# A linear-attention and expert kernel on one core: TensorE's idle products taken out, their PSUM bank given to short products, and a new written-out order of the work

## The chip, the cores and the metric

The kernel runs on one core of a Trainium2 chip. The metric is device time in microseconds. The runs of the kernel before took 575.65, 576.88 and 577.29 us (median 576.88). An execution taken with the profiler took 577.56 us, of which its trace spans 575.7 us.

The engines are named as in the profile: PE is TensorE (PEld its weight loads), DVE is VectorE, ACT is ScalarE, POOL is GpSimd, and SP is SyncE, whose queue issues nearly all transfers.

## What is computed

```python
# q, k, v, alpha: (4, 8, 768, 48); state: (4, 8, 48, 48)
for t in range(768):
    state = alpha[:, :, t, :, None] * state + einsum('bhd,bhe->bhde', k[:, :, t], v[:, :, t])
    y[:, :, t] = einsum('bhd,bhde->bhe', q[:, :, t], state)
x = y.transpose(0, 2, 1, 3).reshape(3072, 384)
g = x @ w_gate                       # 384 x 1536
out = (g / (1 + exp(-g)) * (x @ w_val)) @ w_out
```

The three weight matrices come as 64-bit floats. The kernel cuts them down to 32 bits on the chip.

## The kernel before

**Attention.** The 3072 rows of four batches are worked off in 16 units of 192 time steps (all 8 heads), three chunks of 64 in each. For a unit `u`, words name the steps: `La`, `Lk`, `Lq` and `V` load alpha, k, q and v; `G` and `f` are the backward and the forward scan over alpha on VectorE (with `z` clearing some columns between two units); `mk` and `q` multiply k and q by the decays; `S` are the scores on TensorE, `ma` their causal masks on VectorE; `K` brings k to rows by TensorE transposes (copied out of PSUM by `kc` on ScalarE) in units 0 to 3, and `kr` does the same on VectorE in units 4 to 15; `B` (or `Bw`) makes the carried state, `ad` adds it up, `de` decays it for the next unit; `Y` is the output, rounded to a high part by `yh` and its rest by `yl`. In units 0 to 3 the inputs are turned on TensorE: `p` widens a tile, `T` transposes it into two PSUM banks, and `ea`, `ek`, `cq` copy it out; from unit 4 on VectorE turns them (`tr` for alpha, `tk`, `tq`). `R` and `x` bring the output of units 0 and 1 into the layout of the second part, and from unit 2 on `xr` does it by transfers.

**Experts.** Two units give a block of 384 rows, eight blocks in all. A step is one block and one slice of 128 of the 1536 hidden columns: `g` and `v` are nine products each (three slices of the contraction, times high and low parts), `sl` is the activation on ScalarE, `h` the product with `v` on VectorE, `hh` and `hl` its high and low parts, and `o` nine products into the output. Steps 0 to 6 are block 0, slices 0 to 6; steps 7 to 13 are block 1 with the same slices, and so the same weights; then come the remaining five slices of both, and from step 24 on block after block. `g` and `v` have one PSUM bank each, so `v` of a step waits until `h` of the step before has read that bank.

**Weights.** Group `n` is loaded by `wl`, cut to 32 bits by three VectorE instructions (`w..v0` to `v2`, lines 149, 152 and 155), and split into a high part (`w..a`) and its rest (`w..p`, line 326 on VectorE or GpSimd). Groups 0 to 2 hold one piece, the others two. The cut goes through one of three buffers `t`. Later `wr` and `wc` load and check the ranges of the weights, and `Lc` and `ck` those of alpha.

**The order** of all this is written out as a table: the string `ORDER` is a list of words `engine:name@banks`, and each engine gets its instructions in the order of its words (`t` TensorE, `v` VectorE, `s` ScalarE, `g` GpSimd, `y` SyncE). An engine works its list off in order, and the framework adds the waits that the data and the buffers ask for. The figures behind `@` choose the PSUM banks out of `BANKS`. Of eight banks, three are for short products (`A0` to `A2`), three for the output `o` (`ops0` to `ops2`) and one each for `v` and `g`; until they have their own work, short products use all but `ops2`.

**Idle products.** In `ops2`, before the first `o` needs it, the words `t:3+` or `t:1*` put products of zeros on TensorE, whose result is never read: `dummy32` on 32-bit zeros, `dummy` on 16-bit ones. They stand between the real products of the first units; there are 11 of the first kind and 20 of the second.

Of the kernel before, what the change touches and what calls it, by code (L numbers as in the profile page):

```python
# [48 lines left out]
s:kc1.2 y:wl8 s:kc1.1 v:w3v0 s:qc1 t:4* t:S1@34 v:w3v1 s:ad0.2 v:w3v2 y:wl9 s:ea2 v:de1 s:ad0.0 t:1+ t:3* t:Ta3@02
v:G2 s:kc1.0 t:Y0@16 y:wl10 s:pk2 s:w3a v:f2 g:z2 t:Bw1@5 s:yh0.0 y:V2 s:yh0.1 s:vc1 v:yl0.0 g:w3p s:ad1.0 v:ma1.0  # L50
s:ad1.1 v:ma1.2 v:yl0.1 t:1+ t:2* t:Tk2@14 g:pq2 v:ma1.1 t:R0.2@6 g:w2a v:mk2 s:ad1.2 s:x0.2 v:w2p t:Y1@35 v:w4v0
v:w5v0 t:Tq2@14 v:w5v1 y:V3 s:yh1.0 t:R0.1@6 s:yh1.1 v:w6v0 s:cq2 v:w4v1 s:pk3 t:3* t:K2.1@1 v:w4v2 t:R0.0@4 s:x0.1
s:kc2.1 t:K2.0@6 v:yl1.1 g:q2 s:w4a t:K2.2@1 v:x0.0 v:yl1.0 t:Tk3@45 s:kc2.0 y:Lq3 v:de2 s:kc2.2 y:wl11 t:R1.1@3 s:ea3
t:R1.2@6 v:w6v1 y:wl12 t:R1.0@1 v:w6v2 s:x1.2 t:S2@02 s:vc2 y:wl13 v:G3 t:Bw2@6 s:x1.1 y:wl14 s:x1.0 s:pq3 v:ma2.2
g:qc2 y:Lk4 v:mk3 t:Tq3@13 g:w4p s:ad2.0 s:ad2.1 v:ma2.1 v:ma2.0 v:w7v0 s:ad2.2 v:w7v1 y:wl15 t:Y2@02 v:w7v2 s:cq3
v:de3 s:w7a y:wl16 t:g0 v:f3 g:z3 s:yh2.0 s:yh2.1 s:vc3 t:K3.1@1 t:v0 y:wl17 s:sl0 v:yl2.0 g:q3 s:kc3.1 v:yl2.1 t:g1
y:xr2 v:h0 s:hh0 v:w7p s:qc3 t:S3@01 v:w5v2 s:sl1 t:K3.2@2 v:ma3.2 g:hl0 t:K3.0@3 s:w5a t:v1 v:ma3.1 s:kc3.0 v:ma3.0
s:w6a v:w5p t:o0 s:kc3.2 v:w8v0 v:w6p t:Bw3@0 v:h1 v:w9v0 s:hh1 v:w10v0 y:wl18 t:g2 v:w10v1 s:ad3.0 s:ad3.1 v:w8v1
y:V4 t:v2 s:sl2 v:w8v2 v:w9v1 s:w8a t:Y3@01 v:w9v2 t:g3 v:w8p s:w9a y:V5 s:yh3.0 v:w11v0 s:yh3.1 v:h2 g:hl1 v:yl3.0
t:v3 s:hh2 g:w9p v:yl3.1 s:sl3 v:tk4 t:o1 y:xr3 g:hl2 v:h3 t:g4 s:hh3 v:w12v0 s:vc4 v:hl3 v:w12v1 t:v4 s:sl4 v:w12v2  # L60
t:g5 v:h4 v:w11v1 t:o2 s:sl5 v:w11v2 y:La4 v:w10v2 s:w12a t:o3 s:hh4 v:w12p y:La5 s:w10a t:v5 v:hl4 s:w11a v:w10p t:o4
v:w13v0 v:w13v1 t:g6 v:w13v2 v:h5 g:w11p s:w13a t:v6 s:sl6 v:tr4 s:hh5 g:hl5 t:g7 v:h6 y:Lq4 v:w14v0 s:hh6 t:v7
v:w15v0 s:sl7 v:w15v1 t:o5 v:w13p v:h7 g:hl6 t:g8 s:hh7 v:w14v1 t:o6 v:w14v2 s:sl8 v:w15v2 s:w14a t:v8 s:ot6.0 v:w16v0
s:ot6.1 y:os6.0 v:w16v1 y:os6.1 t:g9 v:h8 g:hl7 s:hh8 v:w16v2 t:v9 s:sl9 v:hl8 s:w16a v:G4 t:g10 s:ot6.2 y:os6.2 t:o7
v:f4 g:z4 s:sl10 t:o8 v:h9 g:mk4 t:v10 s:hh9 g:hl9 v:tq4 t:g11 g:w15a v:h10 y:Lk5 t:o9 s:sl11 g:w15p v:kr4.0 s:hh10
v:kr4.1 t:v11 g:hl10 v:kr4.3 t:g12 g:q4 v:h11 v:kr4.2 s:hh11 t:v12 s:sl12 g:hl11 s:qc4 v:tr5 t:S4@01 g:w16p t:B4@2
v:h12 y:Lq5 v:ma4.2 g:w14p t:o10 v:tk5 s:ad4.0 v:ma4.1 t:o11 y:La6 s:hh12 v:ad4.1 g:hl12 v:ma4.0 t:g13 v:ad4.2 v:w17v0
t:o12 s:sl13 v:w17v1 y:wl19 v:w18v0 t:v13 v:w18v1 v:w18v2 t:Y4@01 v:h13 v:w17v2 s:hh13 t:g14 s:yh4.0 y:V6 v:G5 s:w17a
s:yh4.1 t:v14 s:sl14 v:de5 s:vc5 v:yl4.1 g:hl13 t:g15 v:h14 g:w18a v:yl4.0 s:hh14 t:o13 s:sl15 v:mk5 v:kr5.3 g:hl14
t:v15 s:ot13.0 s:ot13.1 g:w18p v:kr5.0 y:os13.1 t:g16 y:os13.0 v:h15 v:kr5.1 s:hh15 g:w17p t:v16 s:sl16 v:kr5.2 t:g17  # L70
g:hl15 v:h16 v:tq5 s:ot13.2 t:v17 s:sl17 v:f5 g:z5 y:Lk6 t:g18 y:os13.2 t:o14 y:pl18.0 v:h17 v:q5 t:v18 s:hh16 v:w19v0
v:w19v1 v:hl16 t:S5@01 y:xr4 v:w19v2 s:sl18 v:tr6 g:qc5 t:o15 g:w19a g:w19p v:ma5.2 t:o16 s:hh17 v:h18 v:hl17 t:B5@1
v:tk6 s:hh18 g:hl18 t:o17 v:ma5.0 v:ad5.0 y:La7 v:ad5.1 t:o18 v:G6 t:g19 y:Lq6 v:ot18.0 g:mk6 v:ma5.1 t:v19 s:sl19
y:pl18.1 v:ad5.2 y:os18.0 t:g20 v:kr6.3 v:h19 t:Y5@01 v:kr6.1 s:sl20 s:hh19 g:hl19 v:kr6.0 t:v20 s:yh5.0 y:V7 s:vc6
v:de6 t:g21 s:yh5.1 v:ot18.1 v:yl5.1 v:h20 v:tq6 s:sl21 t:v21 s:hh20 y:pl18.2 g:hl20 y:os18.1 v:yl5.0 t:g22 y:Lk7
v:h21 v:f6 g:z6 t:v22 s:sl22 y:xr5 t:g23 v:h22 g:q6 v:kr6.2 t:v23 v:ot18.2 g:qc6 v:tr7 t:o19 v:G7 t:o20 s:hh21
y:os18.2 y:pl23.0 v:tk7 g:hl21 t:S6@01 s:hh22 t:B6@2 g:hl22 s:sl23 v:ma6.2 y:La8 g:mk7 v:h23 t:o21 v:ma6.1 v:ad6.0
y:Lq7 t:o22 v:ma6.0 s:hh23 v:kr7.0 g:hl23 t:g24 v:kr7.2 v:f7 g:z7 t:o23 s:sl24 t:v24 v:ot23.0 v:kr7.3 y:os23.0 t:g25
# [1029 lines left out]
```

## Time and profile before

| what | value |
|---|---|
| median of the runs | 576.88 us |
| the profiled execution, its time | 577.56 us |
| the same, its span in the trace | 575.7 us |
| granted TensorE clock, mean | 0.994 |
| DVE busy over the span | 386.3 us in 596 instructions |
| ACT busy over the span | 248.5 us in 573 instructions |
| POOL busy over the span | 146.4 us in 169 instructions |

A row of the trace in order of time has a start and a length in us, the engine, the line of the program, the operation and its tiles, how many instructions were merged, and in brackets how long the engine idled before and what ended that. A row of a grouped view has busy time in all, the mean of one instruction in ns, and the idle time ahead of the group. A row of a table of stretches has the length and the busy us of each engine in it, the granted TensorE clock, the share of the transfer engines and GB/s. Products on TensorE overlap, so that one's length is more than the distance to the next.

### The profile page before, as it was taken

Reading aid. Unit: us, or ns where it says so; the run is one execution under the profiler, and the core shown is the slowest. Engines: PE = TensorE matmul, PEld = TensorE weight load, DVE = VectorE, ACT = ScalarE, POOL = GpSimd, SP = SyncE. Lnnn points to the kernel's source line nnn. Section 1 sums busy time; section 2 is a strip of 40 time slices with the busy share of each in tenths; the row PEclk is TensorE's granted clock in tenths of the full one; section 3 lists DMA queues with packets and bytes.
Section 4 is the critical chain, followed back from the end, with each engine's and each line's share of the span. In section 5 each row is a group of like instructions: output and inputs, shape, how many; then the busy total and the mean of one; then the engine's idle time right before and its main releaser. Section 6 shows DMA issues by size and latency. Waiting matters only on the chain.

```text
span 575.7 us, 13792 instructions
## 1 busy us (share of the span) xinstructions
PE 556.7 (97%) x5552; PEld 529.0 (92%) x5552; DVE 386.3 (67%) x596; ACT 248.5 (43%) x573; POOL 146.4 (25%) x169
## 2 busy tenths in 40 slices
...
GB/s 205 276 327 219 269 120 142 59 87 98 93 144 155 140 128 105 124 79 149 153 185 198 165 183 135 164 125 125 174 134 126 121 152 66 100 77 48 1 0 47
DMA packets 95367, 77.66 MB, mean 135 GB/s; under 512 B 32832, under 2 KB 92224, under 8 KB 95296
## 3 DMA queue, kind: packets, MB, share of 16 engines
...
## 4 chain that ended last, share of the span: by engine, by line
PE 83%; DMA 8%; SPq 3%; DVE 2%; issue 1%; ACT 1%; DVEq 0%; ACTq 0%
PE ops L735 25%; PE v L703 25%; PE g L703 24%; DMA raw<-in_moe_w_gate_dram 4%; PE A L558 2%; PE s L534 2%; PE y L630 2%; DMA V<-in_v_dram 1%; DMA Le<-in_q_dram 1%; PE y L613 1%; DMA raw<-in_moe_w_val_dram 1%; PE y L614 1%; SPq L687 1%; SPq L281 1%; DVE t L152 1%
## 5 line engine op out<-in xcount | busy, mean ns | idle before, releaser
L703 PE MATMUL v<-xT,w 128*128 128x384 f32 x864 | 167.7, 338 | 2.8 <-DVE h L715 2.8
L703 PE MATMUL g<-xT,w 128*128 128x384 f32 x864 | 167.2, 337 | 0.9 <-ACT h L711 0.9
L735 PE MATMUL ops<-w,hh 128*128 128x384 f32 x576 | 159.0, 338 | 0.3 <-ACT K L498 0.3
L703 PEld LDWEIGHTS v<-xT,w 128*128 128x128 f32 x864 | 150.5, 188 | 4.7 <-DVE h L715 3.9
L703 PEld LDWEIGHTS g<-xT,w 128*128 128x128 f32 x864 | 150.9, 188 | 2.0 <-ACT h L711 1.4
L724 POOL TENSOR_TENSOR hl<-h,hh 128x384 fp32r<-128x384 f32 x67 | 70.6, 1053 | 249.5 <-ACT hh L719 241.7
L715 DVE TENSOR_TENSOR h<-h,v 128x384 f32<-128x384 f32 x96 | 52.9, 551 | 117.8 <-PE v L703 104.5
L719 ACT CAST hh<-h 128x384 fp32r<-128x384 f32 x96 | 49.0, 512 | 150.3 <-DVE h L715 76.7
L735 PEld LDWEIGHTS ops<-w,hh 128*128 128x128 f32 x576 | 105.4, 188 | 1.3 <-ACT K L498 0.6
L735 PE MATMUL ops<-w,hl 128*128 128x384 f32 x288 | 96.8, 336 | 0.0
L711 ACT ACTIVATE h<-g 128x384 f32<-128x384 f32 x96 | 47.0, 489 | 112.2 <-PE g L703 101.0
L509 DVE STREAM_TRANSPOSE K<-Gs 32x384 f32<-32x384 f32 x96 | 54.7, 570 | 5.4 <-PE A L558 3.7
L735 PEld LDWEIGHTS ops<-w,hl 128*128 128x128 f32 x288 | 54.1, 188 | 0.0
L449 DVE TENSOR_TENSOR_SCAN AT<-AT,back 128x771 f32<-128x771 f32 x16 | 29.2, 1824 | 0.7
L440 DVE TENSOR_TENSOR_SCAN Gs<-AT,inj 128x772 f32<-128x772 f32 x16 | 29.4, 1837 | 0.3
L568 DVE TENSOR_TENSOR X<-s,mask 64x384 f32<-64x384 f32 (+1 forms) x48 | 26.0, 551 | 4.8 <-PE s L534 4.2
L724 DVE TENSOR_TENSOR hl<-h,hh 128x384 fp32r<-128x384 f32 x29 | 16.0, 556 | 16.3 <-ACT hh L719 16.2
L453 POOL MEMSET AT<- 128x3 f32 x16 | 1.7, 105 | 90.3 <-DVE AT L449 90.3
L298 ACT ACTIVATE wc<-wc,wbias 128x384 f32<-128x384 f32 x36 | 23.3, 648 | 1.2
L326 POOL TENSOR_TENSOR w<-t,w 128x768 fp32r<-128x768 f32 (+1 forms) x11 | 19.1, 1741 | 15.3 <-ACT w L322 15.1
L468 POOL TENSOR_TENSOR X<-trq,AT 112x768 f32<-112x768 f32 x11 | 19.3, 1752 | 13.4 <-ACT trq L799 6.4
L558 PE MATMUL A<-V,K 64*48 64x48 f32 (+1 forms) x720 | 21.4, 207 | 0.1
...
## 6 DMA issues: line engine op xcount, KB each, us to landing
...
```

The lines of the kernel that those rows point to most:

```text
L298: nc.scalar.activation(dev, dev, AF.Relu, bias=wbias, scale=-1.0, accum_out=wviol[:, 0, i : i + 1])
L440: nc.vector.tensor_tensor_scan(*(x.rearrange("p g t -> p (g t)")[:, ::-1] for x in (Gs, AT, inj)), 0.0, op0=ALU.mult, op1=ALU.add)
L449: nc.vector.tensor_tensor_scan(Af, Af, back[:, 1 : n + 1], back[:, 0:1], op0=ALU.mult, op1=ALU.add)
L509: nc.vector.transpose(out=bass.AP(k0.tensor, k0.offset, [k0.ap[0], (G * 2 * D, NU), (2 * D, G), (1, 32)]), in_=Kg[j * BO + x : j * BO + x ...
L558: nc.tensor.matmul(to[j * BO : j * BO + D, g - gs.start, :], Ks[r, x, g, KC[j]], Vd[r, x, g, VC[j]], start=(x == 0 or not whole), stop=(x ...
L568: nc.vector.tensor_tensor(out=X[r, z, f * GF : (f + 1) * GF, :].rearrange("r g (c t) -> r g c t", c=NU), in0=sps[f][r].rearrange("r g (c t ...
L703: nc.tensor.matmul(pt, wsp[kind, f][a][:, kt * P : (kt + 1) * P], xT[blk][:, b_, kt, :], start=(n == 0), stop=(n == 3 * KT - 1),)
L711: nc.scalar.activation(h, acc.pop(("g", blk, f)), AF.Silu)
L715: nc.vector.tensor_tensor(out=h, in0=h, in1=acc.pop(("v", blk, f)), op=ALU.mult)
L719: nc.scalar.copy(out=hh, in_=acc["h", blk, f])
L724: eng.tensor_tensor(out=hl, in0=acc.pop(("h", blk, f)), in1=hh.bitcast(F32), op=ALU.subtract)
L735: nc.tensor.matmul(ops[blk][i], h[b_][:, i * P : (i + 1) * P], wsp["o", f][a], start=(first and n == 0), stop=(last and n == 2),)
```

## The change

The idle products go: both helpers, the words for them, and the zeros' two names. The bank `ops2` becomes the eighth entry of `BANKS`, so that short products may name it; three do. The string `ORDER` is a new one throughout. No other function changes; lines behind the removed ones move up by 2, and later by 13 to 16.

```diff
 ORDER = """
-y:La0 y:wl0 y:wl1 y:Lq1 y:La1 y:Lq0 y:Lk0 s:pa0 y:V1 t:3+ t:1* t:Ta0@01 v:w0v0 v:w0v1 s:ea0 v:w0v2 v:w1v0 v:w1v1 s:w0a
+y:La0 y:wl0 y:Lk2 y:La2 y:Lq0 y:La1 y:V0 s:pa0 t:Ta0@01 v:w0v0 v:w0v1 s:ea0 v:w0v2 g:w0a v:G0 y:Lk0 s:pq0 y:Lq1 y:V1
...
-    busy32 = inj[:, 0, 0:P]
-    busy = busy32.bitcast(BF16)
...
-    early_ps = ps.tile([P, 512], F32, tag="ops2", name="early_ps")
-
-    def dummy(n):
-
-        for _ in range(n):
-            nc.tensor.matmul(early_ps, busy[:, 0:P], busy.unsqueeze(1).to_broadcast([P, 2, 2 * P]), start=True, stop=True)
-
-    def dummy32(n):
-        for _ in range(n):
-            nc.tensor.matmul(early_ps, busy32[:, 0:P], busy32.unsqueeze(1).to_broadcast([P, 4, P]), start=True, stop=True)
...
-    BANKS = ("A0", "A1", "A2", "ops0", "ops1", "vps", "gps")
+    BANKS = ("A0", "A1", "A2", "ops0", "ops1", "vps", "gps", "ops2")
...
-            if name[-1] in "*+":
-                (dummy32 if name[-1] == "+" else dummy)(int(name[:-1]))
-            else:
-                name, *banks = name.split("@")
-                todo.pop(name)(engines[e], *(BANKS[int(x)] for x in "".join(banks)))
+            name, *banks = name.split("@")
+            todo.pop(name)(engines[e], *(BANKS[int(x)] for x in "".join(banks)))
```

Beside the order itself, the words name another engine in places: unit 7 gets `K` and `kc` (TensorE and ScalarE) in the place of its four `kr` on VectorE; of the `hl`, 57 instead of 67 are on GpSimd and the others on VectorE; of the `mk`, 5 instead of 9; of the `q`, 9 instead of 11; of the `w..p`, 9 instead of 11.

What moves is shown at three places. First SyncE's queue, from its eighth transfer on (before) and from its third on (after): `Le` and `L_71`, `L_72` are tiles of rows of alpha, k or q, `V_77` and `V_78` those of v, and `raw` are weights. Before:

```order
L414 DMA V_78<-in_v_dram 64x4x48 x6
L424 DMA L_71<-in_k_dram 128x2x288
L424 DMA L_72<-in_alpha_dram 128x2x288
L424 DMA L_72<-in_k_dram 128x2x288
L414 DMA V_77<-in_v_dram 64x4x48 x6
L424 DMA L_71<-in_q_dram 128x2x288
L424 DMA L_71<-in_alpha_dram 128x2x288
L281 DMA raw_283<-in_moe_w_gate_dram 128x3x256
L281 DMA raw_286<-in_moe_w_val_dram 128x3x256
L278 DMA raw_286<-in_moe_w_out_dram 128x768
```

After:

```order
L422 DMA L_72<-in_k_dram 128x2x288
L422 DMA L_72<-in_alpha_dram 128x2x288
L422 DMA Le<-in_q_dram 128x2x288
L422 DMA Le<-in_alpha_dram 128x2x288
L412 DMA V_77<-in_v_dram 64x4x48 x6
L422 DMA Le<-in_k_dram 128x2x288
L422 DMA L_71<-in_q_dram 128x2x288
L412 DMA V_78<-in_v_dram 64x4x48 x6
L422 DMA L_71<-in_k_dram 128x2x288
L279 DMA raw_208<-in_moe_w_val_dram 128x3x256
L279 DMA raw_213<-in_moe_w_gate_dram 128x3x256
```

Before, both `V` groups and nine tiles of rows stand between the second weight, which is the third transfer, and the third weight (`raw_283`); tiles of units 2 and 3 come right ahead of it. After, the second and third weights (`raw_208`, `raw_213`) follow each other behind both `V` groups; two tiles of unit 2 have moved to the front, k of unit 0 behind the first `V`, and alpha of unit 3 behind the weights.

Second, VectorE's list at the start, from the second weight's cut on (before) and from the first one's (after). `Gs` is the result of a backward scan, `AT` that of a forward scan, `t` a weight as it is cut, `X` the decayed q or masked scores. Before:

```order
L149 TENSOR_SCALAR t_165<-raw_134 128x384
L152 SCALAR_TENSOR_TENSOR t_165<-raw_134,t_165 128x384
L155 SCALAR_TENSOR_TENSOR t_165<-raw_134,t_165 128x384
L440 SCALAR_TENSOR_TENSOR Gs_171<-AT,inj 128x772
L326 TENSOR_TENSOR w_173<-t_165,w_173 128x384
L446 RECIPROCAL back<-Gs_171 128x4
L449 SCALAR_TENSOR_TENSOR AT<-AT,back 128x771
L466 TENSOR_TENSOR X_103<-pt_2_0_193,AT 112x128x3
L466 TENSOR_TENSOR X_103<-pt_2_1_197,AT 112x128x3
L825 TENSOR_TENSOR Gs_171<-pt_1_0_212,Gs_171 128x4x32x3
L825 TENSOR_TENSOR Gs_171<-pt_1_1_216,Gs_171 128x4x32x3
```

After:

```order
L149 TENSOR_SCALAR t_152<-raw_131 128x384
L152 SCALAR_TENSOR_TENSOR t_152<-raw_131,t_152 128x384
L155 SCALAR_TENSOR_TENSOR t_152<-raw_131,t_152 128x384
L438 SCALAR_TENSOR_TENSOR Gs_160<-AT,inj 128x772
L444 RECIPROCAL back<-Gs_160 128x4
L447 SCALAR_TENSOR_TENSOR AT<-AT,back 128x771
L451 MEMSET AT 128x3
L324 TENSOR_TENSOR w_158<-t_152,w_158 128x384
L464 TENSOR_TENSOR X_103<-pt_2_0_172,AT 112x128x3
L464 TENSOR_TENSOR X_103<-pt_2_1_176,AT 112x128x3
L812 TENSOR_TENSOR Gs_160<-pt_1_0_197,Gs_160 128x4x32x3
L812 TENSOR_TENSOR Gs_160<-pt_1_1_201,Gs_160 128x4x32x3
```

Before, the second weight's cut (`t_165`) stands between the first weight's and the first backward scan. After, that scan follows the first weight's cut, and the second weight is cut later. The decayed q (`X_103<-pt`) and k (the last two rows) follow the forward scan in both.

Third, VectorE's list around `h` of step 6 (`h_6`). `AT<-L_71` is the transpose of alpha for unit 4, the names of `h` give the slice, and the last `h_0` is that of step 7. Before:

```order
L149 TENSOR_SCALAR t_1365<-raw_793 128x768
L152 SCALAR_TENSOR_TENSOR t_1365<-raw_793,t_1365 128x768
L155 SCALAR_TENSOR_TENSOR t_1365<-raw_793,t_1365 128x768
L715 TENSOR_TENSOR h_5_1312<-h_5_1312,v_5_1341 128x384
L375 STREAM_TRANSPOSE AT<-L_71 128x4x6x32
L715 TENSOR_TENSOR h_6_1393<-h_6_1393,v_6_1383 128x384
L149 TENSOR_SCALAR t_1415<-raw_848 128x768
L149 TENSOR_SCALAR t_1429<-raw_882 128x768
L152 SCALAR_TENSOR_TENSOR t_1429<-raw_882,t_1429 128x768
L326 TENSOR_TENSOR w_1381<-t_1365,w_1381 128x768
L715 TENSOR_TENSOR h_0_1431<-h_0_1431,v_0_1419 128x384
```

After:

```order
L149 TENSOR_SCALAR t_1337<-raw_702 128x768
L152 SCALAR_TENSOR_TENSOR t_1337<-raw_702,t_1337 128x768
L722 TENSOR_TENSOR hl_5_1352<-h_5_1275,hh_5_1318 128x384
L152 SCALAR_TENSOR_TENSOR t_1278<-raw_650,t_1278 128x768
L155 SCALAR_TENSOR_TENSOR t_1278<-raw_650,t_1278 128x768
L713 TENSOR_TENSOR h_6_1350<-h_6_1350,v_6_1340 128x384
L324 TENSOR_TENSOR w_1367<-t_1278,w_1367 128x768
L722 TENSOR_TENSOR hl_6_1386<-h_6_1350,hh_6_1384 128x384
L373 STREAM_TRANSPOSE AT<-L_71 128x4x6x32
L713 TENSOR_TENSOR h_0_1381<-h_0_1381,v_0_1371 128x384
```

Before, the transpose of alpha for unit 4 stands ahead of `h_6`; after, it stands behind it, and two `hl` are on VectorE around it.

More of the change, by code (lines that the diff above doesn't have):

```diff
@@ L49 @@
[L49 to L78, printed above, removed]
@@ L134 @@
-v:h95 t:o94 s:hh95 v:hl95 t:o95 s:ot95.0 s:ot95.1 y:os95.0 s:ot95.2 y:os95.1 s:os95.2
+y:La0 y:wl0 y:Lk2 y:La2 y:Lq0 y:La1 y:V0 s:pa0 t:Ta0@01 v:w0v0 v:w0v1 s:ea0 v:w0v2 g:w0a v:G0 y:Lk0 s:pq0 y:Lq1 y:V1
+s:pa1 t:Tq0@01 v:f0 t:Ta1@23 s:vc0 v:z0 v:w0p s:pk0 v:q0 t:Tk0@45 y:Lk1 s:ea1 y:wl1 v:mk0 g:pq1 y:wl2 s:qc0 y:La3 v:G1
+t:Tq1@01 y:wl3 t:K0.2@2 t:K0.1@3 s:kc0.2 t:S0@45 y:wl4 v:f1 s:kc0.1 t:K0.0@2 s:pk1 s:kc0.0 y:Lq2 t:Tk1@36 y:wl5 v:w1v0
+t:Bw0@2 v:ma0.2 g:z1 s:pa2 v:w2v0 s:ek1 y:Lk3 v:w2v1 y:wl6 v:w2v2 s:pa3 v:mk1 t:Ta2@35 s:ad0.0 s:ad0.1 t:Ta3@67
```

146 lines of the change are left out of this document (87 added, 59 removed).

## The prediction

> **What bounds the kernel now.** I read the chain of work that ended last by engine, and then the busy times of every engine by stretches, since an average over a start and a steady state hides both.
>
> ```profile
> PE 83%; DMA 8%; SPq 3%; DVE 2%; issue 1%; ACT 1%; DVEq 0%; ACTq 0%
> ```
> ```profile
> core 0: us, PE busy (x) PEld busy (x) DVE busy (x) ACT busy (x) POOL busy (x), PEclk, DMA share, GB/s
> 0.00:62.00 62.00, 53.59 (x835) 38.80 (x836) 50.56 (x76) 41.33 (x94) 21.07 (x42) 0.97 0.87 258
> 62.00:98.40 36.40, 33.88 (x336) 31.43 (x335) 33.00 (x42) 16.24 (x31) 10.10 (x10) 1.00 0.66 169
> 98.40:200.00 101.60, 101.02 (x952) 98.97 (x953) 94.10 (x141) 28.83 (x60) 43.60 (x39) 1.00 0.42 109
> 200.00:264.00 64.00, 64.00 (x788) 61.58 (x787) 57.31 (x90) 16.01 (x35) 17.03 (x22) 1.00 0.48 112
> 264.00:568.20 304.20, 304.20 (x2645) 298.21 (x2644) 151.36 (x253) 145.64 (x353) 54.63 (x57) 1.00 0.46 120
> ```
>
> From 98.4 us to 568.2 us TensorE idles 0.58 us in all. The work behind 98.4 us is therefore fixed, and the time is decided by **when TensorE becomes full**. That moment is the product behind the seventh `h` (step 6, the last that needs new weights in this block):
>
> ```profile
> 98.39 0.54 DVE L715 TENSOR_TENSOR h<-h,v 128x384 f32<-128x384 f32 x1
> ...
> 98.98 1.83 PE L703 MATMUL v<-xT,w 128*128 128x384 f32 x9 [0.67 <-DVE h L715]
> ```
>
> Up to there VectorE is busy 50.56 + 33.00 = 83.6 of 98.4 us and idles 14.8 us, while TensorE has slack: what it does there includes the idle products. The same stretch, VectorE's rows grouped by line, names most of that idle time:
>
> ```profile
> L149 DVE TENSOR_SCALAR t<-raw 128x768 uint32<-128x768 uint32 (+1 forms) x14 | 9.9, 721 | 8.5 <-DMA raw<-in_moe_w_gate_dram 5.3 <-POOL w L326 1.9 <-DMA raw<-in_moe_w_val_dram 1.2
> ...
> L375 DVE STREAM_TRANSPOSE AT<-L 128x768 f32<-128x768 f32 x1 | 1.6, 1599 | 2.1 <-DMA L<-in_alpha_dram 2.1
> ```
>
> So the start is VectorE's in-order queue, waiting mostly for transfers: 5.3 + 1.9 + 1.2 + 2.1 = 10.5 us.
>
> **The idle products themselves: 0.** They cost TensorE
>
> ```profile
> L777 PE MATMUL early_ps<-inj 128*128 128x512 f32 x22 | 12.9, 716 | 1.2 <-DVE inj L197 1.2
> ...
> L773 PE MATMUL early_ps<-inj 128*128 128x512 bf16 x20 | 5.8, 380 | 0.0
> ```
> ```profile
> L773 PE MATMUL early_ps<-inj x20: 377/379/393, 6.1 to 42.2; 128*128 128x512 bf16 x20
> ```
>
> 18.7 us of busy time, the last of them at 42.2 us, where VectorE is late and TensorE is not. Taking them out frees TensorE where it isn't the bound. What they may have paid for, the clock, is a rival below. The eighth bank is named by three products alone (`Ta3`, `Tq3`, `Y2`), all before the first `o`; later banks are as before, so I give the bank itself nothing either. What counts is the new order.
>
> **What the order moves, up to the seventh `h`.** By the words of the two orders, TensorE has the same real work ahead of `v7`. VectorE gets one more `mk` (+1.0), two more `q` (+2.0) and one more `x` (+0.5), and one transpose and one weight cut slip behind `h6` (-1.6, -1.0); about **+1.0 us** (at 1.03 us for a product out of two banks, row 14.98 below, 0.5 for a copy like the `h` above, 1.6 for the transpose above, 0.96 for a cut, row 43.20's kind below). The waits:
>
> ```profile
> 5.42 5.44 SPq L414 DMA_DIRECT2D V<-in_v_dram  x6
> ...
> 13.53 3.90 SPq L414 DMA_DIRECT2D V<-in_v_dram  x6
> ...
> 18.91 1.06 SPq L281 DMA_DIRECT2D raw<-in_moe_w_gate_dram  x1
> ```
> ```profile
> 5.43 0.45 DVE L149 TENSOR_SCALAR t<-raw 128x384 uint32<-128x384 uint32 x1 [1.38 <-DMA raw<-in_moe_w_gate_dram]
> ...
> 8.31 0.36 DVE L149 TENSOR_SCALAR t<-raw 128x384 uint32<-128x384 uint32 x1 [1.21 <-DMA raw<-in_moe_w_val_dram]
> ...
> 14.98 1.03 DVE L825 TENSOR_TENSOR Gs<-pt,Gs 128x384 f32<-128x384 f32 x2
> ...
> 24.53 1.54 DVE L149 TENSOR_SCALAR t<-raw 128x384 uint32<-128x384 uint32 x1 [3.96 <-DMA raw<-in_moe_w_gate_dram]
> ```
>
> - The third weight is issued at 18.91 and costs 3.96 us at 24.53. Ahead of it stand ten loads of rows (`La0` to `La3`), two weights and two `V` groups; in the new order eight such loads, and the same weights and groups. Two loads fewer are some 1.4 us, and a `V` group without the first one's waiting 1.5 (5.44 against 3.90), so it goes out at about 16 us and, at the 5.6 us that it took (18.91 to 24.53), lands at 21.6. VectorE, through with its second forward scan at 19 to 20, has one cut and one masked product to do before it. I charge 1.5 us in place of 3.96.
> - The cut of the second weight no longer stands between the first weight and the first scan, so the 1.21 goes; the first scan waits for the copy of alpha instead, 0.5.
> - The 1.9 (a buffer `t` held by a subtraction on GpSimd) goes; three buffers remain, but those subtractions that hold them are fewer. The 2.1 goes from this stretch: the transpose of `La4` now stands behind `h6`.
> - New: `Lk0` is now issued behind `V0`, so `mk0` has to come through load, widening and a transpose that nothing warms. I charge 1.7 at 14.98, and 0.9 for `yl1.0`, which waits for a rounding that is behind other copies on ScalarE.
>
> Going: 5.3 less the first weight's own 1.4 (which stays) is 3.9, +1.9 +1.2 +2.1 = 9.1. Coming: 1.5 + 0.5 + 1.7 + 0.9 = 4.6. Net **-4.5**, with both ends: -9.1 if nothing new waits, 0 if as much comes back.
>
> GpSimd stretches VectorE where the two overlap:
>
> ```profile
> 24.16 1.69 POOL L468 TENSOR_TENSOR X<-trq,AT 112x768 f32<-112x768 f32 x1 [2.19 <-ACT trq L799]
> ...
> 42.62 2.09 POOL L468 TENSOR_TENSOR X<-trq,AT 112x768 f32<-112x768 f32 x1 [4.17 <-ACT trq L799]
> ```
> ```profile
> 42.21 0.95 DVE L152 SCALAR_TENSOR_TENSOR t<-raw,t 128x768 uint32<-128x768 uint32 x1
> 43.20 2.32 DVE L155 SCALAR_TENSOR_TENSOR t<-raw,t 128x768 uint32<-128x768 uint32 x1
> ```
>
> The cut at 43.20 took 2.32 against 0.96 for its kind and ended 0.8 after GpSimd's product; the one at 24.53 took 1.54 against 0.36 and ended just behind the other. About 1.3 us each. Of such long products on GpSimd the old order has eight ahead of `h6`, the new one three. Two of the eight hit in this way, so five fewer are worth 5 * 2/8 * 1.3 = **-1.6**; the ends are 0 and five that all hit, 6.5.
>
> Up to `v7` that is -4.5 - 1.6 + 1.0 = **-5.1**: `v7` at about 93.9 instead of 98.98.
>
> **Behind it.** Unit 7 turns its `K` on TensorE now:
>
> ```profile
> 18.04 1.34 PE L493 MATMUL kps<-ident,Gs 112*64 112x112 f32 x12
> ```
>
> **+1.3** in the full stretch, with nothing to hide it; its copies go to ScalarE (busy 28.83 of 101.6) and VectorE loses four `kr`. Between `h6` and `h36`, which is at about 264 us, these come to VectorE or leave it:
>
> ```profile
> L724 POOL TENSOR_TENSOR hl<-h,hh 128x384 fp32r<-128x384 f32 x67 | 70.6, 1053 | 249.5 <-ACT hh L719 241.7
> ...
> L509 DVE STREAM_TRANSPOSE K<-Gs 32x384 f32<-32x384 f32 x96 | 54.7, 570 | 5.4 <-PE A L558 3.7
> ...
> L724 DVE TENSOR_TENSOR hl<-h,hh 128x384 fp32r<-128x384 f32 x29 | 16.0, 556 | 16.3 <-ACT hh L719 16.2
> ```
>
> Seven `hl` from GpSimd (+3.9), two `mk` (+2.0), two weight subtractions (+1.9), two transposes and a cut (+4.2) come; one `q` (-1.0), the four `kr` at two instructions each (-4.6) and three small products (-1.8) leave: 4.6 us more for VectorE, while GpSimd loses 7 * 1.05 for the `hl` alone. VectorE's idle time there was 7.5 + 6.7 = 14.2 us, so it stays in front on average; for single products that it now reaches late I charge **+1.0** (ends 0 and 5). The tail behind 568.2 is the same work.
>
> Sum: -5.1 + 1.3 + 1.0 = **-2.8 us**. The profiled execution took 577.56 us, its span 575.7, and 577.56 is 0.68 above the median of the runs, 576.88; I take the difference from the median: **574.1**.
>
> **Rivals.**
>
> *The clock, slower.* Where TensorE stood idle before, this happened:
>
> ```profile
> 44.70:46.50 1.80, 0.04 (x1) 0.00 (x0) 1.80 (x4) 0.92 (x2) 1.12 (x2) 1.00 0.35 61
> 46.50:47.00 0.50, 0.49 (x3) 0.49 (x4) 0.50 (x2) 0.48 (x2) 0.00 (x0) 0.59 0.44 75
> 47.00:49.50 2.50, 2.50 (x11) 2.44 (x9) 2.40 (x5) 1.73 (x6) 0.00 (x0) 0.50 0.53 83
> ```
> ```profile
> 13.15 0.82 PE L395 MATMUL pt<-ident,wide 128*128 128x128 f32 x6
> 17.18 0.93 PE L534 MATMUL s<-X,Gs 48*64 48x64 f32 x48
> ...
> 22.47 1.28 PE L558 MATMUL A<-V,K 128*48 128x48 f32 x48
> 23.59 0.71 PE L558 MATMUL s<-V,K 128*48 128x48 f32 x24
> 24.13 0.71 PE L558 MATMUL A<-V,K 128*48 128x48 f32 x24
> ...
> 46.51 1.51 PE L395 MATMUL pt<-ident,wide 128*128 128x128 f32 x6 [1.76 <-DVE xT L674]
> ```
>
> After an idle stretch of 1.8 us the granted clock fell to 0.50 for about 3 us, and six transposes took 1.51 us instead of 0.82. Without the idle products TensorE idles that long often in the first 35 us. Units 0 and 1 have on VectorE's way, each, a set of input transposes (+0.7 at half speed), the turning of `K` (1.34 above, so +1.3), the scores (+0.9) and a carry (22.47 to 24.84, so +2.4): 10.6 us together. I have charged 1.7 of it already, which leaves 8.9. If all of it lands the time is 583.0, with two thirds 580.0. It decides from 4.5 us on, half of it, when -2.8 becomes +1.7. [...]
> [...] Chance 0.18.
>
> *Given back, about the same.* The new waits eat most of what goes: a -4.5 that is -2.0 gives 576.6. Or VectorE, with 4.6 us more to do, holds TensorE up to 264 us: the charge of 1.0 becomes 4, which gives 577.1. For: its idle time there is waiting for `v` products, and 14.2 us is all there is. Chance 0.22.
>
> *More.* None of the 4.6 comes and nothing is lost behind `h6`: -2.8 - 4.6 - 1.0 = -8.4, 568.5; with half of that, 571.3. For it speaks the chain of waits, in order of time:
>
> ```profile
> 35.13 8.28 DMA V<-in_v_dram
> ...
> 53.15 9.36 DMA raw<-in_moe_w_gate_dram
> ```
>
> The queue of transfers is a link of it from 35 us on, held by two `V` groups in a row that wait for their buffers, with weights behind them; the new order issues one `V` group there, and eighteen weight transfers before the next. Against it: two of the four new waits are for transfers as well. Chance 0.15.
>
> *That the change doesn't do what it says* can only be so for the bank: three uses.
>
> **Numbers.** The forecast (572 to 576, chance 0.45) is 574.1. The range reaches from just above the full "more", 568.8, to a little over two thirds of the clock rival, 580.4. A measurement of this kernel tells about 0.3%, 1.7 us, from no change: faster is below 575.15. From the cases: faster 0.45 * 0.92 + 0.15 = 0.56, slower 0.19, the same 0.25.
>
> **What would show it.** Right: `v7` begins at 92 to 95 us; VectorE idles 9 to 11 us ahead of `h6`; the third weight's cut waits under 2 us; TensorE idles under 2 us from there to the tail. The clock rival: a granted clock below 0.8 in 10 to 35 us and VectorE's waits there put down to TensorE. Given back: `v7` as said, but TensorE waits for `h` between 100 and 264 us. I am wrong altogether if `v7` begins behind 98 us.

## The result, and the profile after

The kernel got slower. Five runs of the changed kernel have a median of 580.89 us (579.96 to 582.36), the kernel before beside them 576.88 (575.65 to 579.17). The ratio is 1.0071, with a 95% interval from 1.0049 to 1.0094. The prediction was 574.1 with a range up to 580.4, so it is wrong in sign and the time lies outside the range. The profiled execution took 580.9 us, its span is 579.1 (575.7 before), and the granted clock 0.992 (0.994 before).

The share of the chain that ended last, by engine, from the page of the changed kernel:

```profile
PE 77%; DMA 9%; DVE 9%; SPq 2%; issue 2%; ACT 1%; POOL 0%; DVEq 0%; ACTq 0%; POOLq 0%
```

Before, VectorE (DVE) had 2% of that chain; now it has 9%. Where it came in shows in the table of stretches, cut where `h6` starts (93.08), a little behind the first steps that follow it, and at the ends of the stretches that were used before:

```profile
core 0: us, PE busy (x) PEld busy (x) DVE busy (x) ACT busy (x) POOL busy (x), PEclk, DMA share, GB/s
0.00:62.00 62.00, 44.66 (x856) 38.62 (x857) 51.54 (x78) 38.59 (x91) 24.00 (x43) 0.97 0.94 274
62.00:93.08 31.08, 29.58 (x271) 28.28 (x269) 30.00 (x42) 12.40 (x24) 5.71 (x7) 1.00 0.58 142
93.08:105.00 11.92, 10.44 (x51) 10.15 (x51) 8.23 (x12) 3.64 (x7) 3.40 (x2) 0.86 0.42 106
105.00:200.00 95.00, 93.73 (x972) 90.61 (x971) 89.69 (x133) 28.23 (x60) 41.52 (x31) 1.00 0.42 109
200.00:264.00 64.00, 62.87 (x678) 60.00 (x677) 58.38 (x84) 18.00 (x40) 10.95 (x13) 1.00 0.53 125
264.00:572.40 308.40, 308.31 (x2703) 301.25 (x2703) 156.69 (x268) 143.66 (x349) 54.71 (x58) 1.00 0.44 117
```

Up to `h6` VectorE idles 93.08 - 51.54 - 30.00 = 11.5 us, against 14.8 before. Then TensorE idles 1.5 us before 105, and 1.3 and 1.1 in the two stretches behind it, where it had idled 0.6 in all. This is the moment that the prediction spoke of, in order of time: `h6`, the three pieces of `g7` beside it, and `v7`:

```profile
93.08 0.55 DVE L713 TENSOR_TENSOR h<-h,v 128x384 f32<-128x384 f32 x1
```
```profile
92.64 0.76 PE L701 MATMUL g<-xT,w 128*128 128x384 f32 x3 [0.25 <-DMA xT<-X]
94.88 0.76 PE L701 MATMUL g<-xT,w 128*128 128x384 f32 x3 [1.48 <-DMA xT<-X]
95.48 2.99 PE L701 MATMUL v<-xT,w 128*128 128x384 f32 x9
98.27 2.07 PE L701 MATMUL g<-xT,w 128*128 128x384 f32 x9
```

`h6` came 5.31 us earlier than 98.39, but `v7` only 3.50 earlier than 98.98. `g7` is the first product on block 1 and waited for the transfers that carry its `x`. What `v7` then took to the next product was 2.79 us, where 1.67 is usual. The table for that moment has a granted clock of 0.66:

```profile
95.00:100.00 5.00, 5.00 (x20) 5.00 (x21) 2.31 (x4) 0.89 (x2) 1.71 (x1) 0.66 0.37 90
```

The waits of TensorE from 100 to 305 us, by what ended them (total, times, longest). The same view of before has no row:

```profile
engine line waited for: us in total, times, longest us
PE v L701 <- DVE h L713: 1.1, 1, 1.1
PE A L556 <- DVE X L646: 0.8, 1, 0.8
PE ops L733 <- DVE hl L722: 0.5, 2, 0.4
```

To see where the time went, I take three moments from the traces, starts of words on TensorE's queue: `v7`, `g9` (the same words stand ahead of it in both orders) and the last word, `o95`. This table has all kernels of this study, in us:

| kernel | `v7` | `g9` | `g9` to `o95` | span |
|---|---|---|---|---|
| before | 98.98 | 106.96 | 459.51 | 575.75 |
| after | 95.48 | 104.89 | 466.17 | 579.05 |
| e1, `xr3` early | 93.53 | 102.70 | 466.33 | 578.28 |
| e2, new start, old rest | 95.42 | 104.10 | 470.07 | 583.91 |
| e3, old start, new rest | 98.65 | 106.63 | 468.80 | 585.35 |
| e4, before without idle products | 99.01 | 107.02 | 459.42 | 575.57 |
| e5, four words moved | 97.43 | 105.30 | 464.70 | 579.55 |
| e6, four words and `xr3` | 95.07 | 104.09 | 464.59 | 579.01 |
| e7, new to `o23`, old rest | 93.80 | 103.69 | 468.52 | 580.96 |
| e8, unit 7 on VectorE | 95.00 | 103.04 | 472.93 | 586.06 |
| e9, 32 words back on GpSimd | 95.07 | 103.02 | 467.24 | 579.50 |
| e10, e9 with e6 | 94.17 | 103.72 | 466.16 | 579.21 |
| e11, before with two words moved | 97.08 | 104.95 | 459.42 | 572.45 |
| e12, queues cleared | 93.26 | 102.77 | 463.77 | 575.81 |

The change is +3.30 in the span: -2.07 at `g9`, +6.65 from there to `o95`, and -1.28 behind it. I put the last term down to chance: over the fourteen traces what follows `o95` took between 8.0 and 10.3 us, with no pattern by order. So the start gained less than half of the forecast, and the rest, which the prediction gave +2.3, lost 6.65.

### The profile page after: what moved, and what is told of

Same layout as the page of the kernel before. It is cut to its first block, busy times and chain, and to the rows that moved or that the text cites. A ratio compares the mean times of both kernels' runs of the same rounds, so it can differ in the third digit from the quotient of the medians.

```text
span 579.1 us, 13745 instructions
## 1 busy us (share of the span) xinstructions
PE 550.0 (95%) x5522; PEld 529.0 (91%) x5522; DVE 394.5 (68%) x613; ACT 245.4 (42%) x570; POOL 140.3 (24%) x152
## 4 chain that ended last, share of the span: by engine, by line
PE 77%; DMA 9%; DVE 9%; SPq 2%; issue 2%; ACT 1%; POOL 0%; DVEq 0%; ACTq 0%; POOLq 0%
PE ops L733 24%; PE v L701 23%; PE g L701 22%; DMA raw<-in_moe_w_out_dram 3%; PE A L556 2%; DMA raw<-in_moe_w_gate_dram 2%; PE s L532 2%; PE y L628 2%; DMA raw<-in_moe_w_val_dram 2%; DVE t L152 1%; PE pt L393 1%; DVE h L713 1%; DMA V<-in_v_dram 1%; DMA Le<-in_q_dram 1%; DVE K L507 1%
## 5 line engine op out<-in xcount | busy, mean ns | idle before, releaser
L722 POOL TENSOR_TENSOR hl<-h,hh 128x384 fp32r<-128x384 f32 x57 | 68.3, 1199 | 267.4 <-ACT hh L717 266.4
L507 DVE STREAM_TRANSPOSE K<-Gs 32x384 f32<-32x384 f32 x88 | 50.1, 570 | 6.8 <-PE A L556 4.7
L722 DVE TENSOR_TENSOR hl<-h,hh 128x384 fp32r<-128x384 f32 x39 | 22.1, 566 | 30.5 <-ACT hh L717 30.3
L393 PE MATMUL pt<-ident,wide 128*128 128x128 f32 x72 | 13.2, 341 | 12.3 <-ACT wide L381 9.2
L466 POOL TENSOR_TENSOR X<-trq,AT 112x768 f32<-112x768 f32 x9 | 15.9, 1762 | 33.1 <-DMA L<-in_alpha_dram 11.7
L393 PEld LDWEIGHTS pt<-ident,wide 128*128 128x128 f32 x72 | 10.4, 175 | 14.1 <-ACT wide L381 5.6
```

What stands on the lines that cost most here:

```text
L393: nc.tensor.transpose(pt[:, j - js.start, :], Wd.rearrange("p j e c -> p (j e c)")[:, j * P : (j + 1) * P], ident)
L507: nc.vector.transpose(out=bass.AP(k0.tensor, k0.offset, [k0.ap[0], (G * 2 * D, NU), (2 * D, G), (1, 32)]), in_=Kg[j * BO + x : j * BO + x ...
L722: eng.tensor_tensor(out=hl, in0=acc.pop(("h", blk, f)), in1=hh.bitcast(F32), op=ALU.subtract)
```

## Experiments

Each diff is against the order of the changed kernel or of before, as said; `A -> B` means that word A is moved behind or ahead of B on its own queue.

### e1: the transfers of block 1 ahead of the values

Theory at this point: the lead was lost at `g7`. On SP's queue, `xr3`'s ten transfers stood behind the six of `V5`:

```profile
77.93 3.81 SPq L685 DMA_DIRECT2D xT<-X  x6
81.86 4.11 SPq L412 DMA_DIRECT2D V<-in_v_dram  x6
86.14 6.98 SPq L685 DMA_DIRECT2D xT<-X  x10
```
```diff
-y:V5 ... y:xr3
+y:xr3 y:V5
```

> The changed kernel with one word moved: V5 (six transfers of values) stands behind xr3 (the ten transfers that carry x of block 1) on SP's queue, no longer ahead of it. xr3 is then issued some 4 us earlier than at 86.14 us. Theory A (the start's lead of 4.9 us fell to 2.0 at step 7 because g7 waited for these transfers and then ran on a TensorE whose clock had fallen): no wait of PE for xT at g7, v7 begins near 93.5 instead of 95.48 and takes 1.7 us, and the time falls by 2 to 2.8, to 578.1 to 578.9. Theory B (between 100 and 265 us VectorE sets the pace, so a lead that the start hands over is eaten there): the wait at g7 goes too, but the time stays within 1 us of 580.9.

Measured: 581.15 us, ratio 1.0089 (1.0065 to 1.0113). The wait at `g7` is gone and `v7` starts at 93.53, as theory A said, but a wait for `h7` took part of its place one step later:

```profile
93.53 1.84 PE L699 MATMUL v<-xT,w 128*128 128x384 f32 x9 [0.26 <-DVE h L711]
99.42 1.86 PE L699 MATMUL v<-xT,w 128*128 128x384 f32 x9 [0.87 <-DVE h L711]
```

`h7` stands on VectorE behind the transpose of `La4`, which SP issues behind `V5` too. In this trace the kernel is 2.2 us ahead of the changed one at `g9`, and still 2.0 ahead at `o95`: nothing ate that lead, against theory B. Yet the median did not move. The table says why. The start of the new order varies by execution: without this edit `g9` begins at 104.89, 104.10, 105.30, 103.04 and 103.02 (mean 104.07), with it at 102.70, 104.09, 103.69, 103.72 and 102.77 (mean 103.39). The edit is worth 1.7 us at `v7` on the same means and only 0.7 at `g9`, which five runs cannot tell. A single trace gave 2.2, so one trace is no measure of an edit in this stretch.

### e2 and e3: the two orders, halves exchanged

> The order of the change up to and with g9, then all remaining words in the order of before (with the repack of unit 7 by transfers, as before; no idle products). Theory A (the start is worth what is left of it behind step 8, 2.0 us, and the changed kernel loses its time in the new order behind 100 us): 576.9 - 2.0, so 574 to 576. Theory B (what the start of the change leaves undone, the weight groups 13 to 16 and the VectorE work beside them, has to be paid behind 100 us under any order): 577 or more, with TensorE waiting for h between 100 and 265 us. Theory C (the order behind 100 us has nothing to do with it; the missing idle products cost clock): 580 to 581.

> The order of before up to and with g9 without its idle products, then all remaining words in the order of the change (unit 7's repack on TensorE too). Theory A (the new order behind 100 us costs its own 5.3 us at equal TensorE work, and 1.3 for unit 7's turns on TensorE, less 1.2 at the tail): 576.9 + 5.4, so 581.5 to 583. Theory B (the stretch behind 100 us only eats the lead with which it is entered): it ends where the changed kernel ends or 1.5 us ahead of that, 579 to 581.

Measured: 584.79 us, ratio 1.0150 (1.0129 to 1.0172) for e2, and 586.94, ratio 1.0174 (1.0148 to 1.0199) for e3. Both are slower than either whole kernel. e2 has the time and the wait of its theory B (577 or more), though not its "under any order", since the new order goes on from the same `g9` without such a stop; e3 is beyond both of its theories. The traces show why. At the seam of e2 everything stops once, TensorE behind ScalarE and ScalarE behind VectorE:

```profile
114.79 3.25 PE L699 MATMUL g<-xT,w 128*128 128x384 f32 x9 [7.41 <-ACT h L707]
```
```profile
112.34 0.83 ACT L318 CAST w<-t 128x768 fp32r<-128x768 f32 x1 [4.84 <-DVE t L153]
```

The new start leaves VectorE words undone at `g9` that the old one has done there (most cuts of weights 13 to 16, some 8 us by their usual durations; it has done `G4` and `f4` instead), and the exchange puts them all in front of `h9`. On ScalarE the casts `w13a` and `w14a` wait for such cuts, 5.26 and 4.84 us, with `sl9` behind them, for which `g10` waits. Behind that one stop the old order ran without loss: e2 is 7.64 behind the kernel before at `g40` and 7.69 at `o95`. Its `g9` to `o95` is 470.07 only by the seam, which costs 10.4 us over `v9`, `g10` and `o7`.

e3 carries the second finding. It enters the new rest with those cuts already done, and the rest costs 468.80, no less than the 466.17 of the changed kernel. Of the difference, 1.2 us is its own seam at `g9` and 0.9 a new wait at unit 7's first turn of keys. The wait at `v16` is nearly the same as there, 1.1 us:

```profile
147.59 1.83 PE L699 MATMUL v<-xT,w 128*128 128x384 f32 x9 [1.08 <-DVE h L711]
```

This wait has the same size when TensorE comes 2.2 us earlier than in the changed kernel (e1) and when it comes 3.1 us later (e3). If VectorE had no more room and set the pace, an earlier TensorE would wait longer. So this looks like a property of the order around that word, which e5 and e12 test.

### e4: the idle products alone

```diff
-t:3+ t:1* ... t:1+ t:2*
```

> The kernel before without its idle products, the order otherwise untouched. My prediction put them at nothing: 576.4 to 577.4, with the start of h6 within 0.3 us of 98.39. The rival in which the clock is slower without them: cold products and transposes of TensorE cost 3 us or more in the first 40 us, h6 behind 100 and the time at 579 to 582.

Measured: 577.64 us, ratio 1.0012 (0.9989 to 1.0035); `v7` at 99.01 against 98.98. They are worth nothing here, in either direction. But TensorE is slower without them at first. Eighteen input transposes take 4.25 us at 10.73, which is 1.42 for six, where six took 0.82 to 0.88 before. VectorE's second backward scan then waits for ScalarE's copy of them, which it did not before:

```profile
10.73 4.25 PE L391 MATMUL pt<-ident,wide 128*128 128x128 f32 x18 [4.14 <-ACT wide L379]
```
```profile
16.73 1.77 DVE L436 TENSOR_TENSOR_SCAN Gs<-AT,inj 128x772 f32<-128x772 f32 x1 [1.02 <-ACT AT L784]
...
25.05 1.01 DVE L147 TENSOR_SCALAR t<-raw 128x384 uint32<-128x384 uint32 x1 [4.04 <-DMA raw<-in_moe_w_gate_dram]
```

The loss does not last: at 25.05 VectorE waits for the transfer of the third weight as it did before (3.96 us), and that wait covers it. So for the order of before the clock rival falls in its price. TensorE is slower at first, by the durations. That the clock does this is not shown: the column of the granted clock reads 1.00 from 0 to 20 us with and without the idle products. Behind it the clock is as before: from 20 to 30 us it is 1.00 with 6.13 us busy instead of 9.01, and the one stretch of 0.83 in the first 50 us lies at 30 to 40 instead of 40 to 50.

```profile
20.00:30.00 10.00, 6.13 (x162) 5.02 (x162) 5.80 (x10) 7.05 (x21) 3.43 (x3) 1.00 1.01 340
30.00:40.00 10.00, 8.84 (x210) 7.29 (x210) 9.75 (x16) 6.54 (x17) 2.96 (x4) 0.83 1.08 366
```

### e5, e6 and e12: the waits of the rest, word by word

The longest wait behind 100 us, at `v16`, begins with one cut on VectorE. In the changed kernel, VectorE and GpSimd side by side:

```profile
140.41 2.60 DVE L152 SCALAR_TENSOR_TENSOR t<-raw,t 128x768 uint32<-128x768 uint32 x1
143.04 0.96 DVE L155 SCALAR_TENSOR_TENSOR t<-raw,t 128x768 uint32<-128x768 uint32 x1
143.92 0.54 DVE L713 TENSOR_TENSOR h<-h,v 128x384 f32<-128x384 f32 x1
```
```profile
140.14 2.05 POOL L324 TENSOR_TENSOR w<-t,w 128x768 fp32r<-128x768 f32 x1 [0.55 <-ACT w L320]
```

`w17v1` took 2.60 us instead of 0.96 and ended 0.8 after GpSimd's `w16p`; `h15`, ready since 141.7, stood behind it and `w17v2`.

```diff
-v:w17v1 v:w17v2 v:h15 v:kr5.0
+v:kr5.0 v:h15 v:w17v1 v:w17v2
-v:w18v2 v:de5 v:hl15
+v:hl15 v:w18v2 v:de5
-v:f8 v:yl6.1
+v:yl6.1 v:f8
-v:hl32 v:de9 v:hl31
+v:hl31 v:hl32 v:de9
```

> The changed kernel with four words of VectorE moved forward by a few places: h15 (and kr5.0) ahead of w17v1, whose cut took 2.60 us beside a product of w on GpSimd where 0.96 is usual; hl15 ahead of w18v2; yl6.1 ahead of f8; hl31 ahead of hl32. Before each of them TensorE waited (1.39, 0.47 + 0.15, 1.08 and 0.69 us at v16, o15, B7 and o31). Theory A (these four waits are single words that the new order puts behind others, and VectorE has room for them): 3 us less, 577.3 to 578.5, and no wait of PE or PEld for h, hl or X over 0.4 us at these four places. Theory B (VectorE is full from 100 to 265 us, so a word moved forward makes the next one late): waits of the same size at the words behind, 580 to 581.

> The same four moves, and xr3 ahead of V5 on SP's queue as well. If the wait at step 7 and the four waits add up: another 2.0 less than with the four moves alone, 575.2 to 576.7, equal to the kernel before within 0.3%. If the time that is saved at step 7 is not kept in the time of the whole kernel (the run with xr3 alone showed it in its trace, 2.0 us from 105 us to the last product, and not in its median): as with the four moves alone.

Measured: e5 580.80 us, ratio 1.0061 (1.0046 to 1.0077); e6 580.77, ratio 1.0065 (1.0049 to 1.0080). The rest fell from 466.17 to 464.70 and 464.59, half of what theory A wanted. The waits at `o15`, `B7` and `o31` went; two of the four came back next door, at `g17` and `v27`. The one at `g17` has a new name, ScalarE. In e6, ScalarE's row and TensorE's:

```profile
143.64 0.83 ACT L318 CAST w<-t 128x768 fp32r<-128x768 f32 x1 [3.61 <-DVE t L153]
```
```profile
145.32 1.84 PE L699 MATMUL g<-xT,w 128*128 128x384 f32 x9 [1.12 <-ACT h L707]
```

ScalarE stood 3.61 us in front of `w17a`, waiting for the cut `w17v2`, with `hh15` and `sl16` queued behind it. So e12 moves that too:

```diff
-s:w17a s:hh15 s:sl16
+s:hh15 s:sl16 s:w17a
-v:w17p v:w18v1
+v:w18v1 v:w17p
-v:f8 v:ma7.1 v:h26
+v:h26 v:f8 v:ma7.1
```

> The changed kernel with xr3 ahead of V5, the four words moved forward, and three more: the cast w17a behind hh15 and sl16 on ScalarE (with the four words moved, ScalarE stood 3.61 us in front of w17a and TensorE then waited 1.1 us for sl16), w17p behind w18v1 on VectorE, and h26 ahead of f8 (v27 then waited 0.6 us for h26). Theory A (each wait behind 100 us is one word that an in-order queue reaches late, and can be taken out word by word): no wait of TensorE over 0.6 us at g17 and v27, and another 1.5 to 1.8 us less in the trace than with the four words and xr3: a span of 576.5 to 578 and a time of 578 to 580, still behind before by the products that take 0.1 us more beside the units' words and by unit 7's turns on TensorE. Theory B (a wait that is taken out comes back at the next word): the same time as with the four words and xr3, 580 to 581.5.

Measured: 578.96 us (577.53 to 583.50), ratio 1.0049 (1.0026 to 1.0072). What is left of the waits from 100 to 305 us:

```profile
PE v L699 <- DVE h L711: 0.6, 1, 0.6
```

That one is at `v20`, a new place. The rest is down to 463.77, 2.4 less than in the changed kernel, so theory A holds in the trace: these waits come out word by word, if every in-order queue in front of the word is cleared. In the times it is likely but not shown: the interval overlaps that of the changed kernel, and the profiled execution is the fastest of the twelve.

### e7: the seam at a place where both orders have done the same

> The order of the change with xr3 ahead of V5 up to and with o23 (194 us), where both orders have done nearly the same words, then all remaining words in the order of before (unit 7's repack by VectorE, as before). Theory A (the old order loses nothing behind the seam, as the run with the seam at g9 showed from 127 us on, and the new one loses 3.3 there and pays 1.3 for unit 7 on TensorE): TensorE reaches o23 2.0 ahead of before and keeps it, 574 to 575.5, ahead of both kernels. Theory B (the lead is a debt of VectorE words that is paid behind the seam, whatever the order): waits for VectorE between 194 and 270 us of 2 us or more, 576.5 or more.

Measured: 582.87 us, ratio 1.0103 (1.0078 to 1.0128). The time and the wait are those of theory B: one wait of 4.91 us for `h24`, and the words around it, cost 7 us at the seam. But not its reason, a debt "whatever the order": in e1 the new order goes on from the same place without that wait. Behind `g40` the old order again loses nothing: 285.73 us from there to `o95`, 285.69 before.

```profile
199.44 3.25 PE L699 MATMUL v<-xT,w 128*128 128x384 f32 x9 [4.91 <-DVE h L711]
```

### e8: unit 7 back on VectorE

```diff
-t:K7.1 s:kc7.1 ... t:K7.2 t:K7.0 s:kc7.2 s:kc7.0
+v:kr7.1 ... v:kr7.2 v:kr7.0 ... v:kr7.3
```

> The changed kernel with unit 7's repack of keys back on VectorE (four kr7 in the places of the copies kc7, and behind yl6.0) and its twelve turns off TensorE. My prediction: 1.3 us less TensorE work at least; against it 4.6 us more of VectorE between 196 and 207 us. Theory A (TensorE sets the time there): about 579.5, no new wait. Theory B (VectorE is full there): new waits of TensorE for h or X of 2 us or more between 196 and 215 us, and 581 to 584.

Measured: 587.91 us in one run, so theory B, and by more than expected. The four `kr7` stand on VectorE ahead of `f8` and `yl6.1`, for which `B7` waits:

```profile
202.51 2.31 DVE L505 STREAM_TRANSPOSE K<-Gs 32x384 f32<-32x384 f32 x4
204.85 1.77 DVE L436 TENSOR_TENSOR_SCAN Gs<-AT,inj 128x772 f32<-128x772 f32 x1
...
208.61 0.53 DVE L644 TENSOR_TENSOR X<-y,X 112x384 fp32r<-112x384 f32 x1
```
```profile
209.20 1.52 PE L554 MATMUL A<-V,K 64*48 64x48 f32 x32 [5.94 <-DVE X L644]
```

In this one trace, the twelve turns on TensorE save 6.8 us of the rest. In the changed kernel they took 1.02 us, not 1.3.

### e9 and e10: VectorE's load

> The changed kernel with 32 words behind g23 (25 hl, mk8, mk10, mk11, mk13, mk14, q8, q10, q15 among them) back on GpSimd, where they are before; the order untouched. Counted by words, VectorE has 3 to 13 us more to do in the changed kernel than before at equal places of TensorE's order between g26 (200 us) and o35 (275 us). Theory A (that load is what costs the 3 us behind 190 us): the waits at B7 (1.1 us) and o31 (0.7) go and some of the small ones with them, 578 to 579.5. Theory B (the load does not matter, the places of single words do): the wait for yl6.1 at B7 stays, hl31 comes later from GpSimd (1.05 us there, 0.55 on VectorE), 580.5 to 582.

> The run before with the four words moved forward and xr3 ahead of V5 as well. If load, places and step 7 are separate losses (3.3, of which 1.5 by the four moves; 0.9 to 2 at step 7): 576.5 to 578. If one wait only hides the next: as the better of the single runs, 579 to 580.8.

Measured: e9 582.41 us, ratio 1.0111 (1.0081 to 1.0141); e10 581.43, ratio 1.0100 (1.0070 to 1.0130). From 200 to 265 us VectorE is now busy 54.8 of 65 us, where the changed kernel has 58.4 of 64, and yet the rest costs 467.24 in e9 and 466.16 in e10. The stretch in e9:

```profile
200.00:265.00 65.00, 64.08 (x684) 61.26 (x683) 54.79 (x74) 17.17 (x38) 20.74 (x20) 1.00 0.53 125
```

The waits at `B7` (0.7 us) and at `o31` (0.2) stay in part, and a new one of 0.85 us came at unit 7's first turn of keys. So taking load off VectorE did not give the time back, against theory A. The words that left it also end later, since one `hl` takes 1.05 us on GpSimd and 0.55 on VectorE, and the run does not part the two effects. e10 adds nothing to the better of its parts, as its second theory had it.

### e11: a lead in the old order

If leads are kept, the old order should keep one. In the kernel before, the transpose of `La4` waited 2.08 us ahead of `h6`, and `v6` waited for `h5`.

```diff
-y:V5 y:xr3 y:La4
+y:xr3 y:La4 y:V5
-v:w13v0 v:w13v1 t:g6 v:w13v2 v:h5
+v:w13v0 v:h5 v:w13v1 t:g6 v:w13v2
```

> The kernel before, idle products and all, with two words moved at the end of the start: V5 behind xr3 and La4 on SP's queue, so that both are issued some 4 us earlier (in the trace of before the transpose of La4 waited 2.08 us ahead of h6); and h5 ahead of w13v1 (v6 waited for it, g6 took 2.55 us). Theory A (a lead that the start gains is kept by the order of before, which has no wait of TensorE behind 98 us): v7 begins near 97.1, 1.8 earlier than 98.98, and the time is 574.5 to 575.5, ahead of both kernels. Theory B (VectorE is 92 to 95 per cent busy between 100 and 200 us, so a lead of TensorE turns into waits for it): waits for h between 100 and 200 us, 576.3 to 577.3.

Measured: **573.77 us** (572.34 to 574.63, nine runs; the kernel before beside them 576.52), ratio 0.9948 (0.9925 to 0.9971): faster than both kernels. The transpose waits no more, and `v7` follows without a wait at 97.08, where 97.1 was expected:

```profile
94.02 1.61 DVE L374 STREAM_TRANSPOSE AT<-L 128x768 f32<-128x768 f32 x1
95.48 0.53 DVE L714 TENSOR_TENSOR h<-h,v 128x384 f32<-128x384 f32 x1
```
```profile
97.08 1.73 PE L702 MATMUL v<-xT,w 128*128 128x384 f32 x9
```

From there on TensorE does not wait, and `g9` to `o95` is 459.42 against 459.51:

```profile
97.08:200.00 102.92, 102.92 (x1007) 100.54 (x1007) 95.19 (x141) 28.42 (x59) 44.05 (x40) 1.00 0.46 113
200.00:264.00 64.00, 64.00 (x746) 61.90 (x745) 57.41 (x92) 16.35 (x35) 17.03 (x22) 1.00 0.50 114
```

VectorE is 92% busy up to 200 us, and a lead of 2 us passes through. This is the control for the new order: a VectorE that is this busy need not make TensorE wait. Of the 2.7 us in the medians the trace shows 2.0 at `g9`; the rest is within the interval.

## Why the prediction was wrong

**The idle products at 0: right for the old order**, by e4, because a wait for a transfer (4.04 us at 25.05) covers what they save. In the new order that wait is gone, and TensorE is slower, as the clock rival had it. Up to about 20 us six input transposes take 1.51 to 1.54 us instead of 0.82 to 0.88, and the scores of unit 0 1.56 instead of 0.93; the column of the granted clock reads 1.00 there, so that it is the clock is not shown. From 34 to 37.5 us the granted clock is 0.52, and a carry takes 2.16 us instead of 1.28. VectorE waits, among others for the transposes ahead of `mk0`:

```profile
18.93 1.56 PE L532 MATMUL s<-X,Gs 48*64 48x64 f32 x48
...
34.34 2.16 PE L556 MATMUL A<-V,K 128*48 128x48 f32 x48
```
```profile
14.52 1.20 DVE L812 TENSOR_TENSOR Gs<-pt,Gs 128x384 f32<-128x384 f32 x2 [1.59 <-PE pt L393]
...
20.56 0.56 DVE L566 TENSOR_TENSOR X<-s,mask 128x384 f32<-128x384 f32 x1 [0.71 <-PE s L532]
...
37.51 0.55 DVE L566 TENSOR_TENSOR X<-s,mask 64x384 f32<-64x384 f32 x1 [1.19 <-PE s L556]
```

With one more of 0.56 us at 38.61 these waits are 4.1 us, of which the prediction had charged 1.7; the rival had 10.6. What the idle products would be worth in the new order was not tried. At `v7`, behind a wait of 1.48 us for transfers and at a granted clock of 0.66, another 1.1 us went (2.79 us to the next product instead of 1.67).

**The start, -5.1 at `v7`: right up to `h6`, wrong behind it.** `h6` came 5.31 us earlier. The third weight's cut did not wait at all (forecast 1.5), `mk0` waited 1.59 (forecast 1.7), and the cut's buffer on GpSimd held nobody. That the sum met `h6` is in part luck: 2.5 us of waits for TensorE that it did not charge stand against 1.5 us that the third weight did not cost and a stretch by GpSimd that fell by 3.8 us instead of 1.6. What failed is that the prediction took `v7` to follow `h6`. It named no word that is late next. Two were: `xr3` behind `V5`, and `La4` behind `V5`, both on SP's queue. Of the 5.31 us, 3.50 were left at `v7` and 2.07 at `g9` in the profiled execution. e1 shows the first in its trace by taking it out, and the wait for `h7` that then stood behind `La4` is the second. The mean of the five traces without the edit is -2.8 at `g9`, against 106.87 for the three starts in the old order (before, e3, e4). Of the signs that the prediction named, the third weight's came true; `v7` at 95.48 and VectorE's 11.5 us of idle time lie just outside 92 to 95 and 9 to 11, and TensorE idled 4.0 us from `h6` to the tail instead of under 2.

**The step that failed most is "The work behind 98.4 us is therefore fixed", with its charge of +1.0 for single products that VectorE reaches late.** The rest costs 6.65 us more. By the distances between starts of TensorE's words: `g16` took 2.80 us, `o15` 2.01, `g27` 2.61 and `o31` 2.21, where 1.56, 1.57, 1.69 and 1.57 are usual for their kind of neighbours, 3.2 us together; K7's turns 1.02 (the prediction had 1.3). From 265 us on, 75 products up to 400 us take 1.606 on average instead of 74 with 1.598, and 98 up to 566 take 1.585 instead of 101 with 1.580, 1.2 us together. In that stretch 40 products take over 1.62 us instead of 33, most of them next to the words of a unit. The remaining 1.2 us lies in single products between 100 and 265 us. The last two terms were read from the traces and not tried.

The prediction had the mechanism in its rival, TensorE waiting for `h` between 100 and 264 us, but as VectorE's load, weighed by sums: 4.6 us more work against 14.2 us of idle time. e9 and e11 speak against that sum: less load gave nothing back, and 92% load let a lead pass. What e5, e6 and e12 show, for 2.4 of the 6.65 us and in the traces alone, is that the time goes where another word stands in front of the needed one in its queue, on VectorE, and through it on ScalarE. A sum of busy times does not see that; reading the words in front of each `h`, `hl` and `yl` in the new order might have. For the rest of the 6.65 us the cause stays open.

**GpSimd's stretch, -1.6: right in direction, but it was moved, not removed.** For each VectorE instruction that ran beside one of GpSimd, I take its duration less the lower quartile of the same form in both traces. Up to 100 us that is 7.0 us in eight instructions before and 3.2 in four after; from 100 to 160 us it is 2.1 in four before and 5.8 in seven after, because the deferred cuts now meet GpSimd's products there. e5 took one of these away by putting transposes beside `w16p`: `w17v1` took 0.95.

**The tail** was called the same work; it is, and it varies by 2 us over the traces.
